# Decode attention with a cached KV: products with v moved from VectorE to TensorE

## The chip, the cores and the metric

The kernel runs on one core of a Trainium2 chip. The metric is device time in microseconds, the median of several executions. Profile figures come from one further execution taken with the hardware profiler.

## The reference

One token passes four layers: attention, MLP, attention, MLP, both attention layers over the same cache and with the same weights. All is float32: D = 640, 32 heads of 128, 8192 cached positions, 1728 hidden units.

```python
def _A_ref(x, k_cache, v_cache, wq, wo):        # k_cache, v_cache: 1 x 32 x 8192 x 128
    q = (x @ wq).reshape(B, Sq, H, Dh).transpose(0, 2, 1, 3)
    scores = jnp.einsum("bhqd,bhkd->bhqk", q, k_cache) * (Dh ** -0.5)
    p = _softmax(scores, axis=-1)
    o = jnp.einsum("bhqk,bhkd->bhqd", p, v_cache)
    return o.transpose(0, 2, 1, 3).reshape(B, Sq, H * Dh) @ wo
def _B_ref(x, w1, w2):
    return jnp.einsum("bsf,fd->bsd", jnp.maximum(jnp.einsum("bsd,df->bsf", x, w1), 0), w2)

x = x + _A_ref(_layernorm(x), k_cache, v_cache, wq, wo)
x = x + _B_ref(_layernorm(x), w1, w2)
x = x + _A_ref(_layernorm(x), k_cache, v_cache, wq, wo)
x = x + _B_ref(_layernorm(x), w1, w2)
```

## The kernel before

The cache, 268 MB, has to be streamed once for each attention layer. Every head's 8192 positions are laid out as four row groups (32 partitions each) by 2048 columns, and a head is cut into units of columns (`PARTS`, mostly two of 1024; 1024 columns are 4 MB of k and v). All units go through one ring of 3712 columns in SBUF. `pump` issues the next unit's DMA on SyncE's queue (SP) as soon as `place` finds a free stretch, and `release` frees a unit when it has been used. Layer 1 goes through the heads backwards and starts with the units that are still in the ring (`KEPT`), which are loaded only once. SP also issues the weights, in its order of the program: the query weights `wq` and the output weights `wo` of each group of four heads (1280 KB each, one buffer each), and in layer 0 `w1` and `w2`.

For a unit, `scores` (L263) multiplies q, repeated over 32 weight columns, with the keys: four matmuls for 512 columns, one for each row group. VectorE takes the rows' minimum of the negated scores (L272), ScalarE takes the exponential in place in PSUM with its running sum (L274). `values` (L289) is then one VectorE pass for each quarter of the head's 128 dimensions: v, stored with dimensions in the rows, times the exponentials, summed along the row; four passes a unit. A program order written by hand interleaves four of these passes with the next unit's scores and with `chores`, generators that are advanced a step at a time: `heads_out` (rescale four heads' partial sums by their maxima, L304 to L351, then `times_rows` with wo, L239), `queries` of the next group (L220 to L234), and near the end of a layer `mixing` and `before_last`.

`mixing` prepares the product of the last head's part of wo (centred) with `w1`, so that the last head's output `c_o` (L581) can go directly into the MLP's hidden row: it turns that part of wo (L366), centres it (L382, L384) and multiplies it with w1 in four quarters (L397, L404). It starts at the third head from the end. `before_last` adds the first 31 heads to x and multiplies with w1 (L410). After the last unit the rest of the layer follows: the last head's weights by its maxima (L523 to L549), c_o, the hidden row, ReLU, w2 (L239), and x2 (L648). Units listed in `early` have their scores issued before the unit ahead of them is finished.

Of the kernel before, what the change touches and what calls it, by code (L numbers as in the profile page):

```python
# [15 lines left out]
P = 128  # L16
D = 640
# [14 lines left out]
UNIT = 1024  # L32
# [5 lines left out]
RING = 3 * UNIT + 640  # L38
KEPT = [(30, 2), (30, 3), (31, 0), (31, 1), (31, 2), (31, 3)]
# [9 lines left out]
def decode_kernel(ctx: ExitStack, tc: tile.TileContext, x, kv, wq, wo, w1, w2, out):  # L49
# [5 lines left out]
    ps_s = ExitStack()  # L55
    ctx.enter_context(ps_s)

    def cut_banks(n):

        ps_s.close()  # L60
        pool = tc.tile_pool(name=f"ps_{n}", bufs=4 // n, space=bass.MemoryType.PSUM)
        banks[:] = [ps_s.enter_context(pool), n * 512]

    def bank_tile():
        return banks[0].tile([P, banks[1]], F32, name="ps")

    banks = []
    cut_banks(2)
    ctx.enter_context(tc.manual_schedule())
# [4 lines left out]
    order = [(h, i) for h in range(H) for i in range(len(PARTS[h]))]  # L74
    assert KEPT == order[len(order) - len(KEPT) :]
    todo = [(0, s) for s in order] + [(1, s) for s in order[::-1][len(KEPT) :]]
    dram_at = {}
    for h, i in order:
        dram_at[h, i] = (h * COLS + sum(PARTS[h][:i])) * 8 * P
    live = {}  # L80

# [9 lines left out]
    def pump():  # L91
        while todo:
            layer, (h, i) = todo[0]
            n = PARTS[h][i]
            at = place(n)
            if at is None:
                return
            todo.pop(0)
            live[layer, (h, i)] = at, n
            o = dram_at[h, i]  # L100
            nc.sync.dma_start(
                ring[:, 8 * at : 8 * (at + n)],
                kv[o : o + 8 * P * n].rearrange("(p m) -> p m", p=P),
            )

    def key(layer, s):
        return (0, s) if s in KEPT else (layer, s)

    def release(layer, s):
        if layer or s not in KEPT:  # L110
            del live[key(layer, s)]
            pump()
# [3 lines left out]
    def load_wq(g):  # L116
        wq_t[g] = wts.tile([P, NB, HG * DH], F32, name="wq_t")
        nc.sync.dma_start(wq_t[g], wq[g])

    def load_wo(g):  # L120
        wo_t[g] = wts.tile([P, HG, D], F32, name="wo_t")
        nc.sync.dma_start(wo_t[g], wo[g])
# [3 lines left out]
    load_wq(0)  # L126
    pump()
    load_wo(0)

    ones = consts.tile([P, P], F32, name="ones")  # L130
# [10 lines left out]
    fold = consts.tile([P, 32], F32, name="fold")  # L141
    nc.vector.tensor_reduce(fold, ident.rearrange("p (g d) -> p d g", g=4), AX.X, ALU.add)
    all_rows = sel[:, 4:5].to_broadcast([P, P])
# [5 lines left out]
    junk = ps_m.tile([P, UNIT], F32, name="junk")  # L149
# [35 lines left out]
    def spread_of_columns(xc):  # L185
# [6 lines left out]
        nc.tensor.matmul(pv, ones, ss, start=True, stop=True)  # L192
# [22 lines left out]
    def queries(g, xc, r):  # L215

        pq = ps_m.tile([P, 512], F32, name="pm")
# [12 lines left out]
        pt = ps_m.tile([P, 512], F32, name="pm")  # L230
# [17 lines left out]
    st = {}  # L248
    probs = {}

    def scores(step, run):

        L, s, n, e = step
        at, _ = live[key(L, s)]
        nm, _ = st[run[0]]
        j = run.index(s[0])
        ps = bank_tile()
        q = qT[s[0] // HG][:, s[0] % HG : s[0] % HG + 1].to_broadcast([P, 32])
        for b in range(0, n, 512):
            d = min(n, b + 512)  # L260
            for g in range(4):
                k = 8 * at + g * n
                nc.tensor.matmul(  # L263
                    ps[32 * g : 32 * g + 32, b:d],
                    q,
                    ring[:, k + b : k + d],
                    start=True,
                    stop=True,
                )
        probs[L, s] = ps[:, :n]  # L270
        yield
        nc.vector.tensor_reduce(nm[:, j, e : e + 1], ps[:, :n], AX.X, ALU.max, negate=True)  # L272
        yield
        nc.scalar.activation(  # L274
            ps[:, :n],
            ps[:, :n],
            AF.Exp,
            bias=nm[:, j, e : e + 1],
            scale=1.0,
            accum_out=st[run[0]][1][:, 0, j, e : e + 1],  # L280
        )

    def values(step, run, hi):

        L, s, n, e = step
        at, _ = live[key(L, s)]
        j = run.index(s[0])
        v = 8 * at + (4 + hi) * n
        nc.vector.scalar_tensor_tensor(  # L289
            junk[:, :n],  # L290
            ring[:, v : v + n],
            1.0,
            probs[L, s],
            op0=ALU.mult,
            op1=ALU.mult,
            accum_out=st[run[0]][1][:, 1 + hi, j, e : e + 1],
        )

    def heads_out(run, acc, first, last):

        nm, lo = st.pop(run[0])
        J, n = nm.shape[1], nm.shape[2]
        low = work.tile([P, J], F32, name="c_low")
        nc.vector.tensor_reduce(low, nm, AX.X, ALU.min)  # L304
        pt = ps_m.tile([P, 512], F32, name="pm")
        for g in range(4):
            nc.tensor.matmul(  # L307
                pt[:, g * J : (g + 1) * J],
                sel[:, g : g + 1].to_broadcast([P, P]),
                low,  # L310
# [4 lines left out]
        all_low = work.tile([P, J], F32, name="c_all")  # L315
        nc.vector.tensor_reduce(
            all_low, pt[:, : 4 * J].rearrange("p (g j) -> p j g", g=4), AX.X, ALU.min
        )
        d = work.tile([P, J, n], F32, name="c_d")
        nc.vector.tensor_tensor(  # L320
            d, nm, all_low[:, :, None].to_broadcast([P, J, n]), op=ALU.subtract
        )
        w = work.tile([P, J * n], F32, name="c_w")
        nc.scalar.activation(w, d.rearrange("p j e -> p (j e)"), AF.Exp, bias=0.0, scale=-1.0)
        yield
        t = work.tile([P, 5, J * n], F32, name="c_t")
        nc.vector.tensor_tensor(
            t,
            lo.rearrange("p i j e -> p i (j e)"),
            w[:, None, :].to_broadcast([P, 5, J * n]),  # L330
            op=ALU.mult,
        )
        sums = work.tile([P, 5, J], F32, name="c_s")
        nc.vector.tensor_reduce(  # L334
            sums, t.rearrange("p i (j e) -> p i j e", j=J), AX.X, ALU.add
        )
        pt = ps_m.tile([P, 512], F32, name="pm")
        nc.tensor.matmul(pt[:, :J], all_rows, sums[:, 0], start=True, stop=True)  # L338
        for hi in range(4):
            nc.tensor.matmul(  # L340
                pt[32 * hi : 32 * hi + 32, J : 2 * J],
                fold,
                sums[:, 1 + hi],
                start=True,
                stop=True,
            )
        yield
        rl = work.tile([P, J], F32, name="c_r")
        nc.vector.reciprocal(rl, pt[:, :J])
# [375 lines left out]
```

## Time and profile before

| | |
|---|---|
| time, median of 3 runs | 1440.14 us (1439.71 to 1440.53) |
| the profiled execution | 1441.47 us, span 1439.7 us |
| busy: TensorE, its weight loads, VectorE, ScalarE | 618.8, 216.4, 849.8, 170.4 us |
| moved by DMA | 570.78 MB, mean 396 GB/s |
| granted TensorE clock, mean | 0.628 of full |

Rows of the windows view give, for a stretch of time, each engine's busy time, the granted clock, the busy share of the 16 DMA engines and what they moved. Rows of groups give line, engine, operation, out<-in, shapes and count, then busy time, the mean of one in ns, and the idle time before it with what ended it. Rows of the timeline start with the start and the length in us; what ended the idle time before them stands in brackets. A float32 matmul leaves two records in each count.

### The profile page before, as it was taken

To read this page: it belongs to the slowest core of one execution; us is meant where nothing else is said; L and a number is where in the kernel's file an instruction comes from. 1 tells how busy PE (TensorE), PEld (TensorE's weight loads), DVE (VectorE), ACT (ScalarE), POOL (GpSimd) and SP (SyncE) were. 2 spreads that over 40 slices of the span, in tenths; PEclk is the share of its full clock that TensorE was granted. 3 is DMA by queue.
4 is the path that set the end of the run, shared out by engine and by line. 5 is a ranking of instruction groups with operands and counts; after the bars stand their busy time and mean duration, and the time that the engine had idled before them with its cause. 6 is when DMAs were issued, how large, how long until landed. Compare 5 with 4: busy or idle time off the path is not lost. (4 is left out here: it accounts for less than half of the span.)

```text
span 1439.7 us, 10806 instructions
## 1 busy us (share of the span) xinstructions
PE 618.8 (43%) x4140; PEld 216.4 (15%) x4140; DVE 849.8 (59%) x1509; ACT 170.4 (12%) x319; POOL 2.9 (0%) x10
## 2 busy tenths in 40 slices
PE   3343443333434343444574343434434343333476
PEld 1111111011110111112241011111101110111233
DVE  4566566465466655664737756556565665656464
ACT  1111111111111111111101111111111111111110
POOL 0000000000000000000000000000000000000000
PEclk9555665555565566567765665655655656565586
DMA  9999999999999999998517899999999999999980
GB/s 397 438 430 432 428 427 436 428 431 430 431 430 432 432 430 427 435 430 362 217 38 319 359 435 431 429 430 433 432 429 430 432 430 429 431 431 432 429 375 1
DMA packets 24396, 570.78 MB, mean 396 GB/s; under 512 B 2709, under 2 KB 2841, under 8 KB 3097
## 3 DMA queue, kind: packets, MB, share of 16 engines
q1 hardware_dynamic: 24344, 570.09, 92.7%
q8 instruction: 33, 0.54, 0.2%
q14 instruction: 19, 0.15, 0.0%
HBM read 570.08 MB, written 0.00 MB: 396 GB/s over the span
## 5 line engine op out<-in xcount | busy, mean ns | idle before, releaser
L289 DVE SCALAR_TENSOR_TENSOR junk<-ring,ps 128x1024 f32<-128x1024 f32 (+3 forms) x568 | 637.4, 1122 | 203.4 <-ACT ps L274 190.5
L263 PE MATMUL ps<-ring,qT 128*32 128x512 f32 (+1 forms) x2112 | 447.3, 990 | 637.7 <-DMA ring<-in_kv 554.3
L272 DVE TENSOR_REDUCE nm<-ps 128x1 f32<-128x1024 f32 (+4 forms) x142 | 158.8, 1119 | 348.6 <-PE ps L263 348.5
L274 ACT ACTIVATE ps<-ps,nm 128x1024 f32<-128x1024 f32 (+4 forms) x142 | 142.6, 1004 | 1157.2 <-DVE nm L272 1157.2
L263 PEld LDWEIGHTS ps<-ring,qT 128*32 128x32 f32 x2112 | 83.9, 154 | 927.4 <-issue 730.8
L289 DVE DVE_READ_ACCUMULATOR junk<-ring,ps 128x1 f32 x568 | 79.7, 140 | 0.0
L338 PE MATMUL pm<-c_s,sel 128*128 128x4 f32 (+1 forms) x32 | 8.9, 350 | 86.3 <-DVE c_s L334 86.3
L397 PE MATMUL pm<-w_t,wct 128*128 128x448 f32 (+1 forms) x80 | 31.1, 536 | 2.9 <-ACT mix L404 2.4
L220 PE MATMUL pm<-wq_t,ln_xc 128*32 128x128 f32 x640 | 30.4, 356 | 1.7 <-DMA wq_t<-in_wq 1.7
L220 PEld LDWEIGHTS pm<-wq_t,ln_xc 128*32 128x32 f32 x640 | 28.1, 151 | 19.1 <-issue 19.1
L307 PEld LDWEIGHTS pm<-c_low,sel 128*128 128x128 f32 x128 | 23.3, 272 | 31.7 <-issue 31.7
L239 PE MATMUL acc<-wo_t,c_o 128*32 128x160 f32 x496 | 26.9, 373 | 2.8 <-DVE c_o L351 2.8
L307 PE MATMUL pm<-c_low,sel 128*128 128x4 f32 (+1 forms) x128 | 24.7, 316 | 6.7 <-DVE c_low L304 6.7
L274 ACT ACTIVATION_READ_ACCUMULATOR ps<-ps,nm 128x1 f32 x142 | 27.4, 193 | 0.0
L239 PEld LDWEIGHTS acc<-wo_t,c_o 128*32 128x32 f32 x496 | 19.9, 147 | 24.5 <-issue 17.6
L231 PE MATMUL pm<-sel,q_row 128*128 128x4 f32 x32 | 7.5, 304 | 34.0 <-DVE q_row L229 34.0
L338 PEld LDWEIGHTS pm<-c_s,sel 128*128 128x128 f32 x32 | 8.0, 310 | 90.5 <-issue 90.5
L397 PEld LDWEIGHTS pm<-w_t,wct 128*128 128x128 f32 x80 | 14.5, 190 | 20.2 <-issue 11.9
L366 PE MATMUL pm<-ident,wo_t 128*128 128x128 f32 x8 | 2.2, 428 | 28.5 <-DMA wo_t<-in_wo 28.5
L410 PE MATMUL acc<-w_t,ln_xc 128*32 128x448 f32 (+1 forms) x80 | 13.1, 786 | 1.2 <-DVE ln_xc L182 1.2
L239 PE MATMUL junk<-w_t,hT 128*32 128x160 f32 (+1 forms) x224 | 13.2, 388 | 0.0
L231 PEld LDWEIGHTS pm<-sel,q_row 128*128 128x128 f32 x32 | 6.1, 237 | 39.5 <-DVE q_row L229 39.5
(100 smaller groups left out, 118.8 us busy)
## 6 DMA issues: line engine op xcount, KB each, us to landing
ring<-in_kv SPq DMA_DIRECT2D x118, 4096.0 KB, 20.7
wq_t<-in_wq SPq DMA_DIRECT2D x15, 1280.0 KB, 20.4
wo_t<-in_wo SPq DMA_DIRECT2D x15, 1280.0 KB, 17.4
ring<-in_kv SPq DMA_DIRECT2D x7, 2048.0 KB, 14.6
ring<-in_kv SPq DMA_DIRECT2D x8, 1024.0 KB, 10.2
w_t<-in_w SPq DMA_DIRECT2D x1, 4480.0 KB, 30.6
w_t<-in_w SPq DMA_DIRECT2D x1, 4320.0 KB
ring<-in_kv SPq DMA_DIRECT2D x1, 2560.0 KB, 12.6
```

The costliest lines, as they stand in the source:

```text
L220: nc.tensor.matmul(pq[32 * j : 32 * j + 32, :DH], xc[:, c : c + 1].to_broadcast([P, 32]), wq_t[g][:, c, j * DH : (j + 1) * DH], start=(c = ...
L231: nc.tensor.matmul(pt[:, :HG], row, sel[:, :HG], start=True, stop=True)
L239: nc.tensor.matmul(acc[32 * g : 32 * g + 32, :DR], col.to_broadcast([col.shape[0], 32]), wt[:, g * DR : (g + 1) * DR], start=first, stop=last,
L263: nc.tensor.matmul(ps[32 * g : 32 * g + 32, b:d], q, ring[:, k + b : k + d], start=True, stop=True,)
L272: nc.vector.tensor_reduce(nm[:, j, e : e + 1], ps[:, :n], AX.X, ALU.max, negate=True)
L274: nc.scalar.activation(ps[:, :n], ps[:, :n], AF.Exp, bias=nm[:, j, e : e + 1], scale=1.0, accum_out=st[run[0]][1][:, 0, j, e : e + 1],)
L289: nc.vector.scalar_tensor_tensor(junk[:, :n], ring[:, v : v + n], 1.0, probs[L, s], op0=ALU.mult, op1=ALU.mult, accum_out=st[run[0]][1][:, ...
L307: nc.tensor.matmul(pt[:, g * J : (g + 1) * J], sel[:, g : g + 1].to_broadcast([P, P]), low, start=True, stop=True,)
L338: nc.tensor.matmul(pt[:, :J], all_rows, sums[:, 0], start=True, stop=True)
L366: nc.tensor.transpose(pt[:, c * P : (c + 1) * P], wt[:, c * DR : c * DR + P], ident)
L397: nc.tensor.matmul(pt[:, :n], wct[:, c], w1_t[:, c, f : f + n], start=(c == 0), stop=(c == NB - 1),)
L410: nc.tensor.matmul(ph[32 * g : 32 * g + 32, :n], col.to_broadcast([P, 32]), wt[:, f : f + n], start=first, stop=last, skip_group_check=True,)
```

## The change

The exponentials go to SBUF, `turn` brings their keys into the rows with four TensorE matmuls for 512 columns (the exponentials as the 128-column weights, four columns of `sel` moving), VectorE copies the small result, and `values` is 16 matmuls for 512 columns into PSUM (v stored with the keys in the rows; 32 equal weight columns; 128 columns moving). Steps are of at most 512 columns, units hold one or two steps, and each step is released by itself. `combined` rescales one head at a time. `wq` and `wo` are issued on ScalarE's DMA queue after their buffers' last use, and so are `w1`, `w2` (at heads 4 and 7 of layer 0) and a copy of the last head's part of wo (at head 8, in both layers). The mixing starts at head 11, its quarters at heads 12, 16, 20 and 24, one matmul for each step of the list `slow`. First and last units are cut smaller; the ring has the same size.

```diff
-PARTS = {h: [UNIT, UNIT] for h in range(H)}
-PARTS[0] = [256, 256, 512, 1024]
-PARTS[29] = [512, 1024, 512]
-PARTS[30] = [128, 256, 1024, 640]
-PARTS[31] = [1024, 512, 256, 256]
-KEPT = [(30, 2), (30, 3), (31, 0), (31, 1), (31, 2), (31, 3)]
+STEP = 512
+UNITS = {h: [[512, 512], [512, 512]] for h in range(H)}
+UNITS[0] = [[128], [128], [256], [512], [512, 512]]
+UNITS[29] = [[512, 512], [512], [512]]
+UNITS[30] = [[256], [128], [256, 512], [512, 384]]
+UNITS[31] = [[512, 512], [512], [256], [128], [128]]
+KEPT = [(30, 2), (30, 3)] + [(31, i) for i in range(5)]
+MIX_AT = [12, 16, 20, 24]
...
+    def exponentials(st):
+        st.p = work.tile([P, STEP], F32, name="p", bufs=2)
+        nc.scalar.activation(st.p[:, : st.m], st.ps[:, : st.m], AF.Exp, ...)
+    def turn(st):
...
+        for b in range(nb):
+            nc.tensor.matmul(pt[:, 4 * b : 4 * b + 4], st.p[:, b * P : (b + 1) * P],
+                sel[:, :4], start=True, stop=True)
+        st.pT = work.tile([P, STEP // 32], F32, name="pT", bufs=2)
+        nc.vector.tensor_copy(st.pT[:, : 4 * nb], pt[:, : 4 * nb])
+    def values(st):
...
+        for b in range(nb):
+            for g in range(4):
+                v = at + (4 * b + g) * DH
+                nc.tensor.matmul(outs[32 * g : 32 * g + 32, st.slot],
+                    st.pT[:, 4 * b + g : 4 * b + g + 1].to_broadcast([P, 32]),
+                    ring[:, v : v + DH], start=(b == 0), stop=(b == nb - 1), ...)
+        release(st.L, st.s)
...
+    def mixing_quarter(g):
+        for c in range(NB):
+            nc.tensor.matmul(pt[:, :n], wct[:, c], w1_t[:, c, f : f + n], ...)
+            yield
+        nc.scalar.copy(mix[:, f : f + n], pt[:, :n])
...
+        def run_out(k):
+            projected(acc, runs[k], o_cols[k], k == 0, False)
+            yield
+            load_wo(groups[k + 1], nc.scalar)
...
+            if where == 8:
+                nc.scalar.dma_start(mix[:, :D], wo[last // HG][:, last % HG])
+            if where == 11:
+                slow.append(mixing())
+            if where in MIX_AT:
+                slow.append(mixing_quarter(MIX_AT.index(where)))
...
+        for i, unit in enumerate(units):
...
+            work_off(chores, slow)
+            both = i + 1 in ahead and len(unit) + len(units[i + 1]) == 2
+            if i + 1 in ahead:
+                begin(i + 1)
+                if both:
+                    go_on(i + 1)
...
+            for st in unit:
+                turn(st)
+            if i + 1 in ahead and not both:
+                go_on(i + 1)
+            work_off(chores)
+            for st in unit:
+                values(st)
...
+            work_off(chores, slow)
+            if i + 1 not in ahead:
+                begin(i + 1)
+                go_on(i + 1)
```

Here `begin` issues a unit's scores and minima and `go_on` its exponentials. `ahead` holds the last units of a layer (all of the last head's but the first) and the kept units at the start of layer 1.

More of the change, by code (lines that the diff above doesn't have):

```diff
@@ L191, in spread_of_columns @@
         pv = bank_tile()[:, :1]
[L192 removed]
+        nc.tensor.matmul(pv, ss.to_broadcast([P, P]), ones, start=True, stop=True)
         return inv_std(pv)
@@ L246, in times_rows @@
             )
[L248 to L305, printed above, removed]
+    class Step:
+        def __init__(self, L, s, m, e):
+            self.L, self.s, self.m, self.e = L, s, m, e
```

542 lines of the change are left out of this document (283 added, 259 removed).

## The prediction

> **What bounds the kernel now.** I read the page's queues and costliest groups first, then busy time by stage, then the timeline around the stages where transfers thin out.
>
> ```profile
> q1 hardware_dynamic: 24344, 570.09, 92.7%
> ring<-in_kv SPq DMA_DIRECT2D x118, 4096.0 KB, 20.7
> L263 PE MATMUL ps<-ring,qT 128*32 128x512 f32 (+1 forms) x2112 | 447.3, 990 | 637.7 <-DMA ring<-in_kv 554.3
> ```
>
> TensorE idles 637.7 us in front of the scores, 554.3 of them for keys and values to land. A whole 4 MB unit lands 20.7 us after its issue. The stages say where the transfers are not full:
>
> ```profile
> core 0: us, PE busy (x) PEld busy (x) DVE busy (x) ACT busy (x) POOL busy (x), PEclk, DMA share, GB/s
> 0.00:4.00 4.00, 0.77 (x11) 0.77 (x11) 1.13 (x13) 1.28 (x1) 0.70 (x6) 1.00 0.49 141
> 100.00:650.00 550.00, 218.30 (x1410) 69.34 (x1410) 323.84 (x516) 61.73 (x107) 0.00 (x0) 0.60 1.00 431
> 660.00:703.00 43.00, 26.90 (x134) 12.36 (x134) 23.05 (x53) 7.72 (x18) 0.00 (x0) 0.82 0.90 364
> 703.00:757.00 54.00, 36.87 (x368) 19.98 (x372) 28.01 (x102) 5.92 (x18) 1.10 (x2) 0.59 0.08 29
> 757.00:850.00 93.00, 39.64 (x272) 12.04 (x276) 65.51 (x134) 12.90 (x27) 0.00 (x0) 0.61 0.88 367
> 1300.00:1403.00 103.00, 56.02 (x281) 21.91 (x282) 63.62 (x101) 14.06 (x26) 0.00 (x0) 0.68 0.97 414
> 1403.00:1439.70 36.70, 23.74 (x270) 12.75 (x270) 17.52 (x69) 3.52 (x12) 0.55 (x1) 0.69 0.01 2
> 680.00:690.00 10.00, 9.40 (x32) 4.32 (x31) 3.87 (x10) 1.72 (x4) 0.00 (x0) 1.00 0.85 338
> 1410.00:1420.00 10.00, 7.02 (x64) 3.90 (x68) 4.67 (x19) 0.56 (x2) 0.00 (x0) 0.50 0.00 0
> ```
>
> In a full stage the queue moves 431 GB/s at a share of 1.00 while VectorE is busy 59% and TensorE 40%: the stream is the bound and no engine is. Against 431, the time lost (length x (1 - rate/431)) is 2.7 us at the start, 6.7 before layer 0's last byte (660 to 703), 50.4 between the layers (703 to 757), 13.8 while the ring refills (757 to 850), 4.1 before the last byte of all (1300 to 1403) and 36.5 behind it: 114 us. The rest, 1325 us, is bytes, and no part of the change takes bytes away. So the change can win in those 114 us, and lose them and more if an engine becomes slower than the stream.
>
> **The two mixing stalls.**
>
> ```profile
> 665.52 1.09 PE L366 MATMUL pm<-ident,wo_t 128*128 128x128 f32 x4 [19.17 <-DMA wo_t<-in_wo]
> 667.13 0.67 ACT L274 ACTIVATE ps<-ps,nm 128x512 f32<-128x512 f32 x1
> 667.95 0.70 DVE L289 SCALAR_TENSOR_TENSOR junk<-ring,ps 128x512 f32<-128x512 f32 x1 [15.18 <-ACT ps L274]
> 677.64 4.03 PE L397 MATMUL pm<-w_t,wct 128*128 128x448 f32 x10 [0.62 <-ACT mix L404]
> ```
>
> At the third head from the end the mixing wants the last group's wo, which stands in SP's queue behind keys. TensorE waits 19.17 us, the exponential stands behind the mixing's copy on ScalarE, VectorE idles 15.18, nothing is released and the ring starves; then four blocks like the 4.03 us one stand ahead of the scores. The change brings the 320 KB it needs at head 8 and spreads the quarters one matmul at a time over heads 12 to 24. I take away both losses: -6.7 - 4.1 = -10.8 us; at worst (the 4.1 has other parts) -6. The copy is read again in each layer: 2 x 0.33 MB at 431 GB/s, +1.5.
>
> **The unit in the stream.** Per 1024 columns (4096 KB, 9.7 us at 431 GB/s; 10.5 us with an eighth of two weight loads of 1280 KB) VectorE's four products go. TensorE gets eight turning matmuls (weights 128 x 128, four moving columns) and 32 products (32 weight columns, 128 moving).
>
> ```profile
> 398.26 3.64 PE L263 MATMUL ps<-ring,qT 128*32 128x512 f32 x16 [5.17 <-DMA ring<-in_kv]
> 1394.59 1.92 PE L263 MATMUL ps<-ring,qT 128*32 128x512 f32 x16 [1.53 <-DMA ring<-in_kv]
> L307 PE MATMUL pm<-c_low,sel 128*128 128x4 f32 x112 | 21.0, 310 | 0.0
> L599 PE MATMUL ps<-sel,wct 128*128 128x4 f32 x12 | 1.9, 273 | 0.8 <-DVE wct L593 0.8
> L220 PE MATMUL pm<-wq_t,ln_xc 128*32 128x128 f32 x640 | 30.4, 356 | 1.7 <-DMA wq_t<-in_wq 1.7
> 749.32 1.68 PE L220 MATMUL pm<-wq_t,ln_xc 128*32 128x128 f32 x40
> L272 DVE TENSOR_REDUCE nm<-ps 128x1 f32<-128x512 f32 x8 | 5.5, 689 | 3.8 <-PE ps L263 3.8
> L274 ACT ACTIVATE ps<-ps,nm 128x512 f32<-128x512 f32 x8 | 5.3, 664 | 17.9 <-DVE nm L272 17.9
> L274 ACT ACTIVATION_READ_ACCUMULATOR ps<-ps,nm 128x1 f32 x142 | 27.4, 193 | 0.0
> L234 DVE COPY qT<-pm 128x4 f32<-128x4 f32 x16 | 2.5, 156 | 1.4 <-PE pm L231 1.4
> ```
>
> A matmul here leaves two records. Turning has its own shape in L307: 21.0/56 = 0.375 us each, 3.0 a unit; the queries' shape is that of the products: 30.4/320 = 0.095, 3.0 a unit. Scores are 447.3/2112 x 16 = 3.4. With about 1.1 a unit of chores (three wide matmuls a head; queries and output rows every fourth head) that is 10.5 us at the clock of now (0.60), against 10.5 of stream: at that clock TensorE would be even with it. At full clock (1.92 for the scores; L599's 1.9/6 = 0.32 for turning; 0.084 or less for products, from 1.68/20) it is 1.9 + 2.5 + 2.7 + 0.9 = 8.0; wholly cold some 11.3 (10.5 x 3.64/3.4). Within a unit TensorE also waits for an exponential, at most 0.69 + 0.66 + 0.19 = 1.5 us, and as the two steps overlap I take half, 0.7.
>
> Which clock? The rows show that it follows density: 1.00 where TensorE was busy 9.40 of 10 us, 0.50 where 7.02; the same scores took 3.64 us after a wait of 5.17 and 1.92 after one of 1.53. A TensorE that falls behind runs products into scores, over 6 us without a gap, and wakes its clock; then it catches up. I therefore cost the middle of the stream at nothing: 8.7 us hidden by 10.5, with 20.7 - 9.7 = 11 us of queued transfer to cover a late release. Without that cover each 0.1 us a unit costs 12.4 us over 124 loaded units. The Trainium skill speaks against it: its page "TensorE: Matmul & The Clock Gate", section "A second HAM failure mode: psum-queue depth-cycling", says that short idles between groups of matmuls that cycle through PSUM banks let the clock swing between half and full rate, at the cost of warming up again and again. By the dense row a unit takes 8.7 us; by that rule, taken as the middle of warm and cold, about 10.4 (estimate), which leaves the sum as it is but without slack. No run so far shows which holds for this mixture.
>
> VectorE falls to two reductions and two copies a unit (1.7 us), ScalarE stays at two exponentials (1.7): neither binds.
>
> **Weights on ScalarE's queue.** With the share at 1.00 a second queue adds no bandwidth: 0. A load there waits for the matmuls that read the old weights, and exponentials stand behind it; between lie at least eight turning matmuls (3.0 us) against 1.3 of output rows, so 0, and up to 3 us each, 30 times, if not; the 11 us of queue cover that too.
>
> **The two ends.**
>
> ```profile
> 734.26 0.16 DVE L581 TENSOR_TENSOR c_o<-pm,c_r 128x1 f32<-128x1 f32 x1 [0.36 <-PE pm L573]
> 747.29 0.08 DVE L648 DVE_READ_ACCUMULATOR xr<-junk,ln_r,xr 128x1 f32 x1
> 756.84 46.58 SPq L101 DMA_DIRECT2D ring<-in_kv  x8
> 1428.23 0.16 DVE L581 TENSOR_TENSOR c_o<-pm,c_r 128x1 f32<-128x1 f32 x1 [0.36 <-PE pm L573]
> 1436.78 0.08 DVE L648 DVE_READ_ACCUMULATOR xr<-junk,ln_r,xr 128x1 f32 x1
> L410 PE MATMUL acc<-w_t,ln_xc 128*32 128x448 f32 (+1 forms) x80 | 13.1, 786 | 1.2 <-DVE ln_xc L182 1.2
> 730.13 2.45 PE L410 MATMUL acc<-w_t,ln_xc 128*32 128x448 f32 x24
> L239 PE MATMUL acc<-wo_t,c_o 128*32 128x160 f32 x496 | 26.9, 373 | 2.8 <-DVE c_o L351 2.8
> 1421.54 0.16 DVE L523 TENSOR_REDUCE c_low<-nm 128x1 f32<-128x4 f32 x1
> 1422.99 0.20 ACT L549 ACTIVATE c_w<-c_d 128x4 f32<-128x4 f32 x1 [0.89 <-DVE c_d L547]
> ```
>
> From the last byte to the last head's output (c_o) it is now 31.4 us in layer 0 (703 to 734.4) and 25.4 in layer 1; VectorE has 2048 columns or more of products left. Afterwards TensorE has them. The scores of the 512 unit, which stand ahead of the turning of the 1024 before it, start when it lands, 4.9 us before the last byte, or about 3.9 with a signal's delay (my estimate). Then, at mean durations: scores of 1024 columns 3.4; sixteen turnings 6.0; products of 2048 columns 6.1; the head before, three wide matmuls, 1.1; its rows 24/496 x 26.9 = 1.3; layer norm some 1.3 (estimate: three wide matmuls and their hand-overs); the hidden rows 13.1/2 = 6.5; eight wide matmuls for the last head 3.0; two chains from minimum to weight, 1.65 each (1421.54 to 1423.19), 3.3: 32.0, so c_o at +28. At full clock: 1.9 + 5.1 + 5.4 + 1.0 + 1.0 + 1.0 + 2.45 x 5/3 = 4.1 + 2.5 + 3.3 = 25.3, less if products go at the scores' 0.06 (1.5): about +20. I take +23.5, as the stretch is dense but starts cold: -7.9 in layer 0 (from -11.4 to -3.4), -1.9 in layer 1 (from -5.4 to +2.6). From c_o to the layer's end nothing changes but the clock (13.0 and 8.5 us now): 0, within 4.5 either way.
>
> Layer 1's first release comes 9.5 us after the layer's result (747.37); a first unit of 128 columns instead of 256 and one product instead of four shorten that by an estimated 1.5 (0 to 3). The refill then waits on releases: now 13.8 us are lost. The new pieces fit the ring worse: walking the placement rule through its releases, head 29's first piece waits for 896 columns of head 30, and head 28's first for a piece of head 29 that layer 1 itself loaded. With 4.1 us per 512 columns on TensorE (the middle of 4.7 at the clock of now and 3.6 at full clock) I get loads of 128, 256, 512, 512 and 1024 columns at 0, 4.7, 10.4, 17.0 and 26.1 us and of 1024 at 43.7 and 56: 33 us of transfer in 56, 23 lost; with 3.0 (all three passes at the full clock of the scores) 9; I take 16, as nothing waits for a landing there and the clock should rise: +2.2, from -5 to +9.
>
> **Sum.** -10.8 + 1.5 - 7.9 - 1.9 - 1.5 + 2.2 = -18.4. The profiled execution took 1441.5 around its span of 1439.7, 1.3 over the median of 1440.1; from 1441.5 it becomes 1423.1, and against the median 1421.7, the forecast.
>
> **Rivals.** (1) Slower: TensorE becomes the stream's bound. For it: 10.5 us a unit at today's clock before any wait, and a turning matmul moves only four columns, which may not count as density. Against: the 9.40-of-10 row at clock 1.00. It decides from a mean clock of about 0.68 downwards in mid-layer, where the work is 9.8 (between 8.0 at 1.00 and 10.5 at 0.60, linear in 1/clock) and the exponential's wait fills the 10.5. At today's clock a unit takes 11.2: 0.7 x 124 = 87 us, less 18.4, 1509; wholly cold (12.0) 1608; 0.15 a unit eats the gain. The Trainium skill's same page, "Part 4: PE-mode transpose", states that transposes in that mode do not count as busy for the clock gate; turning here is an ordinary matmul, so the rule may not reach it, and no run here shows it. (2) The ends swap VectorE for TensorE one for one, and only the mixing pays: 1440.1 - 10.8 + 1.5 = 1431. For it: the +28 above. (3) No change: the refill eats the rest (16 to 30 us lost in it), or starvation at 660 comes back elsewhere: 1438 to 1443. Against it, head 8's load has eight heads of slack.
>
> **How the numbers follow.** Forecast 0.64, rival (1) 0.17, (2) 0.13, (3) 0.06. All good ends together, -10.8 + 1.5 - 11.4 - 5.4 - 3 - 5 - 4.5 = -38.6, give 1402; all poor ones, -6 + 1.5 - 3.4 + 2.6 + 9 + 4.5 = +8.2, give 1448, and I stop at 1446, which takes in (2) and (3); what is left out is most of rival (1). The forecast's own range is 1402 to 1437. Faster by over 0.2% (2.9 us; about what a measurement of this kernel can tell from no change): 0.63 + 0.13 = 0.76; within it 0.07; slower 0.17.
>
> **What would show it.** Right: 431 GB/s from 100 to 1390 but for the layers' change, no dip at 660 or 1300, a granted clock above 0.65 in the stream with TensorE at 65 to 85%, c_o some 20 to 28 us behind each last byte, TensorE in the chain at the end. Wrong: scores that no longer wait for landings in mid-layer, fewer than 425 GB/s there, exponentials that wait behind ScalarE's transfers, or a refill that loses over 25 us.

## The result, and the profile after

The changed kernel took 1560.22 us (median; 1555.95 to 1568.6) against 1440.32 for the kernel before on the same chip: a ratio of 1.084, 95% interval 1.0795 to 1.0886. It is slower by 120 us; the forecast was 1421.7, faster by 18.4. Rival (1), TensorE as the stream's bound, is what happened. Ratios and their intervals, here and below, leave out executions in a slower state of the chip (one of the run with two banks and one of the control further down), while the medians count them, so a ratio can differ a little from that of the medians.

The page of the kernel after: engines, the stream's queue and the weights' queue, the shares of the chain that ended last, then the costliest TensorE groups (busy us in total, mean ns | idle us before them and what ended it) and the whole units' transfers with their us from issue to landing.

```profile
PE 1263.2 (81%) x14484; PEld 880.2 (57%) x14484; DVE 385.0 (25%) x1350; ACT 223.1 (14%) x617; POOL 2.9 (0%) x10
...
q1 hardware_dynamic: 20456, 524.38, 81.0%
q10 hardware_dynamic: 4608, 46.37, 7.2%
...
PE 72%; DVE 12%; DMA 10%; issue 5%; ACT 2%; SPq 0%; ACTq 0%; DVEq 0%
...
L313 PE MATMUL outs<-ring,pT 128*32 128x128 f32 x8192 | 418.9, 385 | 38.3 <-DVE pT L305 37.5
...
L297 PE MATMUL outs<-sel,p 128*128 128x4 f32 x2048 | 325.5, 281 | 74.3 <-DVE pT L305 41.0
...
L263 PE MATMUL ps<-ring,qT 128*32 128x512 f32 (+3 forms) x2144 | 327.7, 735 | 21.7 <-DMA ring<-in_kv 21.2
...
ring<-in_kv SPq DMA_DIRECT2D x117, 4096.0 KB, 16.4
```

The scores waited 554.3 us for landings before; now it is 21.2. TensorE is busy 81% of the span and carries 72% of the chain: the data is there and TensorE is late. A unit lands 16.4 us after its issue instead of 20.7, so the queue behind the stream is shorter. The stages of the kernel after (us, busy time by engine, granted clock, DMA share, GB/s):

```profile
core 0: us, PE busy (x) PEld busy (x) DVE busy (x) ACT busy (x) POOL busy (x), PEclk, DMA share, GB/s
100.00:640.00 540.00, 438.91 (x5054) 307.58 (x5050) 133.35 (x451) 78.72 (x214) 0.00 (x0) 0.74 0.98 408
...
700.00:900.00 200.00, 159.74 (x1676) 107.85 (x1679) 46.30 (x175) 24.49 (x76) 1.10 (x2) 0.65 0.51 206
900.00:1380.00 480.00, 399.48 (x4706) 278.43 (x4702) 123.62 (x420) 73.77 (x200) 0.00 (x0) 0.76 0.98 409
1380.00:1554.10 174.10, 143.31 (x1640) 99.76 (x1632) 43.85 (x163) 22.73 (x65) 0.55 (x1) 0.72 0.69 282
```

The same cuts of the kernel before, the two that are not at full rate:

```profile
700.00:900.00 200.00, 95.08 (x746) 37.24 (x746) 126.72 (x285) 24.84 (x55) 1.10 (x2) 0.60 0.70 292
...
1380.00:1439.70 59.70, 39.58 (x348) 19.58 (x346) 31.49 (x91) 7.75 (x19) 0.55 (x1) 0.77 0.38 161
```

Time lost, length x (1 - rate/431): 28.8 us from 100 to 640 and 24.5 from 900 to 1380 where the kernel before lost 0 and 3.3 (its 428); 104.4 from 700 to 900 against 64.5; 60.2 behind 1380 against 37.4. So of 113 us (the spans differ by 114.4), 50 arose in the steady middle, 40 around the change of layers and 23 at the end.

What TensorE waited for (total us, times, longest):

```profile
PE pm L373 <- DVE c_o L367: 76.2, 62, 2.1
PE pm L330 <- DVE c_low L328: 55.0, 64, 0.9
PE outs L297 <- DVE pT L305: 41.0, 114, 0.5
PE outs L313 <- DVE pT L305: 37.5, 141, 0.3
PE outs L297 <- ACT p L280: 32.5, 41, 1.7
...
DVE c_o L363 <- PE outs L313: 140.2, 59, 3.0
```

These five make 242 us, 1.9 for each of the 128 units' worth (1024 columns) of keys and values. L330 waits for the minimum of a head's maxima. The two rows that wait for the copy of the turned weights (L305) come from their place in the outputs' bank: the next turning (L297) waits until the first result has been copied out of it, and the products (L313), which write to the same bank, wait for the copy of the second. (With a bank of its own for the turned weights, in the runs with wide turning below, this last wait falls from 37.5 to 5.4 us.) The last row is VectorE: before it reads a head's partial outputs it waits for products that run into the same banks, and the head's two summing matmuls (L373) then wait for VectorE at the front of TensorE's queue.

### The profile page after: what moved, and what is told of

Read it like the earlier page. It is cut to its first block, busy times and chain, and to the rows that moved or that the text cites. A ratio compares the mean times of both kernels' runs of the same rounds, so it can differ in the third digit from the quotient of the medians.

```text
span 1554.1 us, 31963 instructions
## 1 busy us (share of the span) xinstructions
PE 1263.2 (81%) x14484; PEld 880.2 (57%) x14484; DVE 385.0 (25%) x1350; ACT 223.1 (14%) x617; POOL 2.9 (0%) x10
## 4 chain that ended last, share of the span: by engine, by line
PE 72%; DVE 12%; DMA 10%; issue 5%; ACT 2%; SPq 0%; ACTq 0%; DVEq 0%
PE outs L313 25%; PE outs L297 18%; PE ps L263 17%; DMA ring<-in_kv 10%; DVE c_o L367 4%; DVE pT L305 3%; PE px L420 3%; DVE nm L273 2%; PE pm L373 2%; ACT p L280 2%; PE pm L330 1%; DVE c_o L363 1%; PE px L221 1%; PE acc L433 1%; PE px L240 1%
## 5 line engine op out<-in xcount | busy, mean ns | idle before, releaser
L313 PE MATMUL outs<-ring,pT 128*32 128x128 f32 x8192 | 418.9, 385 | 38.3 <-DVE pT L305 37.5
L297 PEld LDWEIGHTS outs<-sel,p 128*128 128x128 f32 x2048 | 310.7, 230 | 177.0 <-ACT p L280 110.3
L297 PE MATMUL outs<-sel,p 128*128 128x4 f32 x2048 | 325.5, 281 | 74.3 <-DVE pT L305 41.0
L313 PEld LDWEIGHTS outs<-ring,pT 128*32 128x32 f32 x8192 | 344.3, 156 | 68.2 <-DVE pT L305 49.8
L263 PE MATMUL ps<-ring,qT 128*32 128x512 f32 (+3 forms) x2144 | 327.7, 735 | 21.7 <-DMA ring<-in_kv 21.2
L280 ACT ACTIVATE p<-ps,nm 128x512 f32<-128x512 f32 (+3 forms) x268 | 179.0, 668 | 1105.8 <-DVE nm L273 1004.0
L273 DVE TENSOR_REDUCE nm<-ps 128x1 f32<-128x512 f32 (+3 forms) x268 | 178.9, 668 | 544.5 <-PE ps L263 544.3
L263 PEld LDWEIGHTS ps<-ring,qT 128*32 128x32 f32 x2144 | 76.4, 136 | 146.7 <-issue 120.7
L305 DVE COPY pT<-outs 128x16 f32<-128x16 f32 (+3 forms) x268 | 46.6, 174 | 393.1 <-PE outs L297 392.6
L373 PE MATMUL pm<-sel,c_o 128*128 128x1 f32 x124 | 29.1, 304 | 76.2 <-DVE c_o L367 76.2
L330 PEld LDWEIGHTS pm<-sel,c_low 128*128 128x128 f32 x128 | 19.4, 191 | 112.9 <-DVE c_low L328 111.3
L373 PEld LDWEIGHTS pm<-sel,c_o 128*128 128x128 f32 x124 | 23.8, 240 | 81.5 <-DVE c_o L367 81.5
L367 DVE SCALAR_TENSOR_TENSOR c_o<-outs,c_w,c_o 128x128 f32<-128x128 f32 x194 | 68.1, 351 | 6.9
L330 PE MATMUL pm<-sel,c_low 128*128 128x4 f32 x128 | 24.9, 265 | 55.0 <-DVE c_low L328 55.0
L280 ACT ACTIVATION_READ_ACCUMULATOR p<-ps,nm 128x1 f32 x268 | 51.7, 193 | 0.0
L420 PE MATMUL px<-w_t,wct 128*128 128x448 f32 (+1 forms) x80 | 47.3, 680 | 0.0
## 6 DMA issues: line engine op xcount, KB each, us to landing
ring<-in_kv SPq DMA_DIRECT2D x117, 4096.0 KB, 16.4
```

The source lines that it names most:

```text
L263: nc.tensor.matmul(st.ps[32 * g : 32 * g + 32, :n], q, ring[:, at + g * n : at + (g + 1) * n], start=True, stop=True,)
L273: nc.vector.tensor_reduce(nm[:, st.e : st.e + 1], st.ps[:, : st.m], AX.X, ALU.max, negate=True)
L280: nc.scalar.activation(st.p[:, : st.m], st.ps[:, : st.m], AF.Exp, bias=nm[:, st.e : st.e + 1], scale=1.0, accum_out=l[:, st.e : st.e + 1],)
L297: nc.tensor.matmul(pt[:, 4 * b : 4 * b + 4], st.p[:, b * P : (b + 1) * P], sel[:, :4], start=True, stop=True,)
L305: nc.vector.tensor_copy(st.pT[:, : 4 * nb], pt[:, : 4 * nb])
L313: nc.tensor.matmul(outs[32 * g : 32 * g + 32, st.slot], st.pT[:, 4 * b + g : 4 * b + g + 1].to_broadcast([P, 32]), ring[:, v : v + DH], st ...
```

## The experiments

**The second queue.** All transfers of weights go back to SP's queue.

```
-            load_wo(groups[k + 1], nc.scalar)
+            load_wo(groups[k + 1], nc.sync)     # and every other nc.scalar.dma_start
```

> The changed kernel with wq, wo, w1, w2 and the copy for the mixing issued on SyncE's queue again. Theory T (TensorE is the bound in mid-layer: about 9.5 us of work a unit at a granted clock of 0.74 and some 2 us of hand-over waits make 11.3 us, against 10.5 of stream): no change, 1545 to 1575 us, and 400 to 405 GB/s from 1000 to 1400 as before. Rival D (the 403 GB/s at a DMA share of 0.97 come from two queues that share the engines): 431 GB/s in mid-layer again and about 1490.

1550.73 us, ratio 1.0772 (1.0732 to 1.0812), and from 1000 to 1400 the same rate as the kernel after, 403 GB/s in both. The second queue is not the cause; at most it costs some 10 us of the 120, as the two runs' ranges (1545.69 to 1557.94, and 1555.95 to 1568.6) just touch. The Trainium skill, page "DMA: Bandwidth & Descriptors", section "Issuing engines are not separate DMA queues", says that transfers issued by different engines share the same DMA engines; the equal rates agree.

**Less work, or fewer waits.** First, half of the turning goes.

```
-        nb = st.m // P
+        nb = max(1, st.m // P // 2)      # in turn(); values() reads column 4 * (b % half) + g
```

> The changed kernel with half of the turning left out: each step turns only its first half of 128-column blocks and uses them for the second half too, so part of the products is taken with the wrong weights. Theory T: turning takes 325 us of TensorE in 268 steps; half of it is about 1.25 us a unit, which brings the unit from 11.3 to about 10.1, under the stream's 10.5: mid-layer back to 425 to 431 GB/s, and 1475 to 1490 us. Rival D (queues): 1550 to 1560, still about 403 GB/s. Rival C (turning lowers the clock because it does not count as dense): more than that, the granted clock rises from 0.74 to above 0.85 and products take about 2 us for 64 records in place of 3.3.

Second, the summing matmuls of a head go one step later, behind other TensorE work:

```
         del heads_of[h]
+        yield
         pt = ps_m...
```

> The changed kernel with one more step between VectorE's rescaling of a head's output and the two matmuls that sum it, so that TensorE does not stand waiting for VectorE. Theory T: TensorE waits 76 us for it in 62 heads, 0.6 us a unit; mid-layer gains most of that, 1500 to 1525 us. Rival C (the clock is what matters): the wait is filled but the clock falls as before, gain under 25 us. Rival D: no change.

Third, the turned weights leave the outputs' bank every other time (one bank fewer for scores):

```
-    turned = [outs[:, SLOTS, 16 * i : 16 * i + 16] for i in range(4)]
+    tr = ps_m.tile([P, 512], F32, name="tr")
+    turned = [tr[:, :16], outs[:, SLOTS, :16]]    # ps_s: bufs 3 -> 2
```

> The changed kernel with the results of turning put alternately into a PSUM bank of their own and into the bank of before (the scores get two banks in place of three for it). Theory T: the second turning of a unit no longer waits for the copy of the first (41.0 us in 114 waits of 0.36 us); as TensorE is the bound, the time falls by about as much: 1515 to 1530 us. Rival: such short waits are covered by others (the next exponential), gain under 15 us.

Fourth, the second and third together:

> The changed kernel with both hand-over edits: the later summing matmuls and turning into two PSUM banks. Theory T: in mid-layer the stream is the bound again with some slack, 428 to 431 GB/s, so this adds less than the two gains apart (72 and 63 us): 1460 to 1475 us. What stays over the early mixing alone (1422) is the layers' ends, where TensorE does products and turning one after another.

The windows 1000 to 1400 of half turning, late output, two banks, and the last two together, in this order:

```profile
1000.00:1400.00 400.00, 306.47 (x3905) 192.81 (x3904) 108.62 (x377) 65.58 (x178) 0.00 (x0) 0.80 1.00 425
```
```profile
1000.00:1400.00 400.00, 334.53 (x4072) 236.03 (x4072) 109.00 (x368) 65.16 (x176) 0.00 (x0) 0.80 1.00 425
```
```profile
1000.00:1400.00 400.00, 343.37 (x4062) 235.93 (x4054) 107.36 (x362) 63.86 (x173) 0.00 (x0) 0.76 0.99 420
```
```profile
1000.00:1400.00 400.00, 331.26 (x4110) 231.93 (x4106) 109.45 (x371) 65.17 (x177) 0.00 (x0) 0.79 1.00 425
```

Half turning took 1464.61 us (ratio 1.0182, 1.0159 to 1.0205), the late output 1487.68 (1.0336, 1.0321 to 1.0352), two banks 1497.12 (1.0381, 1.0361 to 1.0402; the row above is from an execution of 1510.7) and the last two together 1476.7 (1.0264, 1.0236 to 1.0292). Each alone brings the middle from 403 to 420 or more: at 403 a unit with its share of weights (4416 KB) takes 11.2 us where the stream needs 10.5, so 0.7 us less is enough. The clock of half turning rose to 0.80 in this window, short of the 0.85 that rival C named. All three gained more than expected: 96 us and not 70 to 85, 73 and not 35 to 60, 63 and not 30 to 45. That is also more than the 50 us lost in the middle, so a part of it comes from the layers' ends. The late output's gain is not the wait's alone, because the clock in its window is 0.80 where the kernel after has 0.76. The two together gained only 11 more than the late output alone, and just missed the expectation: once the stream is the bound again, the rest is not in the middle.

**Issuing the next scores earlier**, in every unit instead of the last ones of a layer, without and with the late output:

```
+        ahead = set(range(1, len(units)))
         chores, slow = [], []
```

> The changed kernel with every unit in the list ahead: a unit's scores stand before the turning of the unit ahead of it, in the whole of both layers. Theory T: TensorE has the next scores to do while the exponentials are made, so the waits on ScalarE (142 us with the weight loads) and on the minima go; mid-layer back to 425 GB/s or more, 1490 to 1510 us in all, the rest of the loss at the layers' ends. Rival: a unit's buffer is now freed only after the next one has landed, about 9.7 us later than now, which leaves no unit queued: transfers thin out and nothing is gained, 1540 or more.

> The two edits together: every unit ahead, and one step more between VectorE's rescaling and its two matmuls. Theory T: mid-layer is the stream's at 428 to 431 GB/s with slack for TensorE; what stays is the ends, 45 to 50 us over the kernel before: 1475 to 1488 us. If the ends were long only because of single units that wait for their own exponentials, heads 29 and 30 now overlap too and it would be 1465 or less.

1642.35 us (ratio 1.1421, 1.1363 to 1.1479) and 1651.43 (1.1457, 1.1419 to 1.1494): the first as its rival said, the second a miss. The scores of the run without the late output:

```profile
L263 PE MATMUL ps<-ring,qT 128*32 128x512 f32 (+3 forms) x2144 | 363.8, 808 | 244.9 <-DMA ring<-in_kv 244.2 <-DVE qT L235 0.5
...
ring<-in_kv SPq DMA_DIRECT2D x117, 4096.0 KB, 14.7
```

Its scores wait 244.2 us for landings, while the turning and the products that would release the ring stand behind them: the ring has less queued (14.7 us from issue to landing), and an order that fills an exponential's wait opens a longer one.

**The clock.** A prelude to the kernel before, on TensorE alone: 120 turning matmuls (four moving columns), 60 groups of four products, 120 turning matmuls.

> The kernel before with a prelude on TensorE that nothing waits for but a copy: 120 turning matmuls (128 x 128 weights, four moving columns), 60 groups of four products (32 weight columns, 128 moving), 120 turning matmuls. Rival C (turning does not count as dense): in the first stretch the granted clock stays at 0.5 and a turning matmul takes about 0.46 us throughout; in the products it rises to 1.0; in the third stretch it falls back to 0.5. Theory T without C: the clock rises to 1.0 within the first stretch and stays there, 0.26 us a turning matmul.

Its timeline (start, length) with one row for each stretch, and windows within the second and third stretch:

```profile
1.58 51.33 PE L148 MATMUL pm<-sel,ident 128*128 128x4 f32 x240 [1.58 <-DVE mhalf L138]
52.85 15.01 PE L151 MATMUL acc<-ident,sel 128*32 128x128 f32 x480
67.79 49.33 PE L153 MATMUL pm<-sel,ident 128*128 128x4 f32 x240
```
```profile
57.00:65.00 8.00, 8.00 (x304) 8.00 (x296) 0.00 (x0) 0.00 (x0) 0.00 (x0) 1.00 0.02 4
...
70.00:105.00 35.00, 35.00 (x166) 35.00 (x166) 0.00 (x0) 0.00 (x0) 0.00 (x0) 0.50 0.00 0
```

The total, 1536.21 us in one run, contains the prelude. The products run at clock 1.00. Turning, with TensorE busy 35.00 of 35 us, runs at 0.50: a full TensorE does not hold its clock on this shape, 49.33/120 = 0.41 us each.

The first stretch is turning as well, and there the clock column shows 1.00 where 0.5 was expected. The column cannot be used there: the trace holds no clock record before 56.4 us, and where it has none the column reads 1.00. The spacing of the matmuls tells the clock instead. From record to record the first stretch takes 213.3 ns, just as the third does after its clock has fallen at 70.0 us; before that fall the third takes 112.7. The first clock record of the trace is a rise to 1.00, 3.5 us into the products, and the products, at 52.0 ns a record before it, take 27.0 after it. So turning was slow from the start and did not wake the clock in 51 us of unbroken work; the products did.

In the kernel after it looks like this (start, length, last wait):

```profile
1002.55 1.95 PE L313 MATMUL outs<-ring,pT 128*32 128x128 f32 x64 [0.27 <-DVE pT L305]
...
1020.01 1.87 PE L297 MATMUL outs<-sel,p 128*128 128x4 f32 x8
1022.24 1.84 PE L297 MATMUL outs<-sel,p 128*128 128x4 f32 x8 [0.36 <-DVE pT L305]
1024.35 3.64 PE L313 MATMUL outs<-ring,pT 128*32 128x128 f32 x64 [0.27 <-DVE pT L305]
```

The same 64 records of products take 1.95 us where the clock is up and 3.64 behind a cold turning. So the turning was made wide: its four columns repeated 32 times as moving columns, into a bank of its own, of which four columns a block are copied.

```
+    tr = ps_m.tile([P, 512], F32, name="tr")      # ps_s: bufs 3 -> 2
+    wide = sel[:, None, :4].to_broadcast([P, 32, 4])
-                pt[:, 4 * b : 4 * b + 4],  ...  sel[:, :4],
+                tr[:, P * b : P * b + P],  ...  wide,
```

> The changed kernel with each turning matmul given 128 moving columns (the same four, 32 times) in place of four, into one bank of its own; only four are copied, the result is the same. It makes turning dense at the price of more columns. Rival C (it is the sparse turning that cools the clock): the granted clock in mid-layer rises from 0.76 to 0.9 or more, products fall from a mean of 51 ns a record to about 32, and though turning is no shorter the time falls to 1480 to 1510 us. Theory T without C (only waits and the amount of work count): the clock stays at 0.72 to 0.78, turning gets longer and the time is 1560 to 1620 us.

The control keeps bank and copy, and moves four columns:

```
-                tr[:, P * b : P * b + P],  ...  wide,
+                tr[:, P * b : P * b + 4],  ...  sel[:, :4],
```

> The wide turning had two edits in it: the bank of its own and the 128 moving columns. Here the bank stays and the moving columns are four again; nothing else differs. If the columns did it through the clock: a mean clock of 0.73 to 0.76, products of 385 us or more instead of 263.8, 410 to 422 GB/s from 1000 to 1400, and 1500 to 1535 us, as the run with two places for the turned weights took 1497.1 and this one has a single place with a wait of about 40 us for its copy. If the bank did it: 1460 to 1470 us with the wide clock.

Wide, then the control:

```profile
L297 PE MATMUL tr<-sel,p 128*128 128x128 f32 x2048 | 325.6, 305 | 76.4 <-DVE pT L305 40.5 <-ACT p L281 35.6
...
L316 PE MATMUL outs<-ring,pT 128*32 128x128 f32 x8192 | 263.8, 281 | 6.3 <-DVE pT L305 5.4 <-DVE wct L577 0.8
...
1000.00:1400.00 400.00, 299.97 (x4136) 197.51 (x4136) 107.98 (x368) 65.39 (x177) 0.00 (x0) 0.92 1.00 426
```
```profile
L296 PE MATMUL tr<-sel,p 128*128 128x4 f32 x2048 | 332.8, 285 | 72.2 <-DVE pT L304 40.7 <-ACT p L280 31.2
...
L315 PE MATMUL outs<-ring,pT 128*32 128x128 f32 x8192 | 405.2, 376 | 6.3 <-DVE pT L304 5.4 <-DVE wct L576 0.8
...
1000.00:1400.00 400.00, 344.70 (x3947) 235.81 (x3946) 103.50 (x350) 61.29 (x166) 0.00 (x0) 0.73 0.97 408
```

Wide: 1460.38 us (ratio 1.0147, 1.0131 to 1.0163), better than expected. Control: 1540.39 (1.0631, 1.0571 to 1.0691), just over its expectation. The rows of waits are alike; the moving columns alone are worth 80 us by the medians and 70 by the ratios. 32 times as many columns cost no more time (325.6 against 332.8), and not only because the clock is higher: at a clock of 1.00 four turning matmuls take 1.05 us wide (the wide run at 1014.71) and 1.03 narrow (the kernel after at 1001.26). The products, which are the same instructions in both runs, fall from 405.2 to 263.8, with the clock at 0.92 in place of 0.73. This pair shows the clock as a cause; the bank of its own, with four columns, is worth only the 20 us (30 by the ratios) between the control and the kernel after.

**What the ends cost.** The wide turning with the late output, and that with the pieces (256 columns at the smallest) of the kernel before:

> Wide turning and the later summing matmuls together. With C: TensorE has slack in mid-layer (431 GB/s), the ends get shorter by the warmer clock: 1445 to 1470 us. Without C: about 1490 to 1540.

```
-UNITS[31] = [[512, 512], [512], [256], [128], [128]]
+UNITS[31] = [[512, 512], [512], [256], [256]]     # heads 0 and 30 likewise; six kept pieces
```

> The wide turning with the late output reader took 1455.5 us, 33 more than the early mixing alone, most of it at the layers' ends. Here it gets the pieces of the first and the last two heads back from the kernel before (256 columns at the smallest instead of 128, six kept pieces instead of seven). If the small pieces cost what they cost in the kernel with the early mixing alone (10 us), 1443 to 1448. If the TensorE tail needs them, each piece of 256 adds a later start of its last products, 1456 to 1465.

1455.47 us (ratio 1.011, 1.0096 to 1.0125) and 1441.76 (1.0006, 0.9994 to 1.0019), first the new pieces, then the old:

```profile
700.00:900.00 200.00, 151.73 (x2130) 103.60 (x2122) 56.62 (x212) 30.60 (x91) 1.10 (x2) 0.87 0.70 288
...
1380.00:1454.00 74.00, 56.12 (x651) 36.99 (x650) 17.72 (x75) 7.91 (x25) 0.55 (x1) 0.76 0.36 153
```
```profile
700.00:900.00 200.00, 151.59 (x2140) 103.61 (x2136) 57.50 (x213) 31.35 (x91) 1.10 (x2) 0.90 0.75 311
...
1380.00:1439.00 59.00, 45.81 (x542) 28.52 (x542) 13.79 (x60) 5.81 (x18) 0.55 (x1) 0.80 0.26 111
```

The losses there go from 66.4 + 47.7 to 55.7 + 43.8: 14.6 us, and the medians differ by 13.7, a little more than the 10 that were expected. The small pieces of the change were a cost of their own, most of it in the refill: from the first release to 900 us 19.8 us are lost with the new pieces and 7.4 with the old (373 GB/s from 753, and 409 from 755). With them undone, the clock held and the reader moved, the changed kernel is level with the kernel before; but it has the early mixing in it, so the products on TensorE still eat all that the mixing brings.

**The mixing alone.** The kernel before with the last group's wo copied at head 8 (on SP's queue) and the mixing at head 11; then with smaller ends (128 columns) in the first and the last head; then in the first head only.

```
-                if where == H - 3:
+                if where == 8:
+                    nc.sync.dma_start(mix[:, :D], wo[last // HG][:, last % HG])
+                if where == 11:
                     chores.append(mixing(last))

-PARTS[0] = [256, 256, 512, 1024]
+PARTS[0] = [128, 128, 256, 512, 1024]     # second and third run
-PARTS[31] = [1024, 512, 256, 256]
+PARTS[31] = [1024, 512, 256, 128, 128]    # second run only, KEPT + (31, 4)
```

> The kernel before with one part of the change alone: the copy of the last head's wo is loaded at head 8 and the mixing is done from head 11 on, w1 and w2 at heads 4 and 7; all on SyncE's queue, products still on VectorE. My prediction's term: 10.8 us lost at 660 to 703 and 1300 to 1403 come back, 1.5 are paid for the copy: about 1431 us, and no dip in transfers before a layer's last byte. Rival: the dips come from the ring's shape at the end of a layer, not from the mixing: 1440 to 1443.

> The kernel before with early mixing (1422 us) and, as in the change, the last 256 columns of head 0 and of head 31 cut into two units of 128. It asks whether the smaller last units are worth something where VectorE does the products. The work that VectorE has left after the last byte is the same, each further unit adds some 1.5 us of fixed costs to it, and the first release of layer 1 comes about 1.5 us earlier: 1420 to 1426 us.

> The early mixing alone, with smaller pieces in the first head only (128, 128, 256, 512, 1024), so that what the last head's pieces and the longer kept list cost stays out. If the refill of the ring was what the smaller ends lost, 1419 to 1424 us; if the short pieces themselves cost (more instructions on VectorE at the end of layer 1), 1427 to 1432.

The mixing alone took 1422.43 us (ratio 0.9876, 0.9862 to 0.9891), about 9 better than the 1431 expected; with smaller ends in both heads 1432.68 (0.9955, 0.9942 to 0.9968; a miss), and in the first head only 1423.98 (0.9885, 0.987 to 0.99). Two windows of the mixing alone, and the last row of its layer 0 output:

```profile
1300.00:1385.00 85.00, 35.12 (x202) 9.53 (x194) 53.16 (x82) 11.05 (x19) 0.00 (x0) 0.60 0.99 426
1385.00:1421.00 36.00, 22.48 (x260) 13.26 (x260) 17.05 (x69) 2.69 (x10) 0.55 (x1) 0.67 0.03 10
```
```profile
721.01 0.16 DVE L583 TENSOR_TENSOR c_o<-pm,c_r 128x1 f32<-128x1 f32 x1 [0.36 <-PE pm L575]
```

The dip at 1300 is gone (426 GB/s where 414 were), and since VectorE is no longer behind when the last byte lands, c_o follows it by 23.7 us in layer 0 (697.5 to 721.2) instead of 31.4. (The stream does not end sharply: the last packets of its queue end at 701.9 here and at 704.8 in the kernel before, and from those c_o follows by 19.2 us instead of 29.6.) This is the fastest version, faster than both kernels. The smaller last head and its longer kept list cost most of the 10 us: with the first head's pieces alone, 1.5 remain, which is hardly more than the runs scatter.

## Why the prediction was wrong

**The step that failed** is "I therefore cost the middle of the stream at nothing: 8.7 us hidden by 10.5". It cost 50 us there. The work term was right: 9.3 us of TensorE a unit (333.47 busy of 400 us from 1000 to 1400, x 11.2), where I had 9.2 at that window's clock of 0.76 by my own line. In part that is luck, because the line's end for the full clock was too slow: its row at 749.32 ran at a clock of 0.73, and at 1.00 the products of a unit take 1.95 us (the row at 1002.55) where I had 2.7. Two things beside the work term were wrong.

First, the waits. I counted the exponential alone and took 0.7 us a unit. It measured 0.25 (32.5/128). Four hand-overs with VectorE that I did not count measured 1.6: two for the place of the turned weights in the outputs' bank, one for the combining of a head's outputs, and one for the minimum of its maxima. Taking away the largest (late output) returns the stream to 425 GB/s.

Second, the clock. I argued that "a TensorE that falls behind runs products into scores ... and wakes its clock; then it catches up". TensorE did fall behind, and the clock stayed at 0.74 to 0.76: the turning between them lets it fall however dense it is (probe), so falling behind had no end. Rival (1) named the reason, "which may not count as density", and I gave it 0.17; but its threshold of 0.68 was too low, because its wait was. With 1.9 us of waits 8.6 are left of 10.5, which by my line between 8.0 at 1.00 and 10.5 at 0.60 asks for a clock of about 0.86; wide turning has 0.92 and streams at 426. Either remedy alone brings the stream back (425 GB/s with the late output, 426 with wide turning), so the runs do not divide the 50 us between waits and clock. The rival's price, 1509 at the old clock, put 87 us on the middle, where 50 were measured, and nothing on the layers' change and the end, where 63 were.

The Trainium skill, page "TensorE: Matmul & The Clock Gate", section "A second HAM failure mode: psum-queue depth-cycling", has the clock swing between half and full rate, and the trace agrees (1.00 from 1002.5 to 1004.5 us, 0.50 from 1020 to 1028); the 10.4 (estimate) that I drew from it is to be set against 9.3 of work and 1.9 of waits. The short idles that it gives as the reason are not what holds the clock down here: wide turning and its control have nearly the same waits (76.4 and 72.2 us before turning, 6.3 before the products in both) and clocks of 0.92 and 0.73, and the probe cools without a gap. Its "Part 4: PE-mode transpose" speaks of transpose mode; the probe shows the same for an ordinary matmul with four moving columns, at 0.50.

**The ends.** I forecast c_o 23.5 us behind each last byte; it is 45.5 in layer 0 (737.6 to 783.1) and 33.9 in layer 1 (1504.1 to 1538.0):

```profile
746.83 1.06 PE L263 MATMUL ps<-ring,qT 128*32 128x512 f32 x8
...
782.92 0.16 DVE L616 TENSOR_TENSOR c_ol<-pm,c_r 128x1 f32<-128x1 f32 x1 [0.68 <-PE pm L612]
...
1505.48 1.06 PE L263 MATMUL ps<-ring,qT 128*32 128x512 f32 x8
...
1537.80 0.16 DVE L616 TENSOR_TENSOR c_ol<-pm,c_r 128x1 f32<-128x1 f32 x1 [0.68 <-PE pm L612]
```

From those scores to c_o are 36.2 and 32.5 us, against 32.0 in my sum at mean durations: that sum was near, and my step down toward the full clock was not, as the clock there is 0.71 and 0.72. The stretch also starts 9.2 and 1.4 us after the last byte and not 3.9 before it, since TensorE comes in with a backlog. In layer 0 that goes with the clock: counted from the last packet, the same scores start 7.6 us after it in the kernel after (746.8 against 739.2), 8.4 after it in the control (741.5 against 733.1), but 1.9 before it with wide turning (705.8 against 707.7). With the late output alone it is still 6.6 after. From that packet to c_o the control takes 44.0 us and wide turning 29.4.

**The refill** was sized at 16 us lost, bounds 9 to 23. The first 97 us of it:

```profile
803.00:900.00 97.00, 79.86 (x830) 54.56 (x825) 22.72 (x76) 13.55 (x39) 0.00 (x0) 0.62 0.67 269
```

That is 36.5 us lost. The clock is a part of it, since the same pieces lose 22.7 us with wide turning (330 GB/s from 759 to 856, clock 0.89) and 35.6 in its control (273 from 799 to 896, clock 0.61). The pieces are another part: the old ones take 12.4 us off the refill of the wide turning with the late output.

**Right:** the second queue at nothing (same rate without it); the first release, 7.6 us after the layer's result (795.3 to 802.89) and 9.5 before, -1.9 where I had -1.5; the direction of the mixing, though -9.3 with the copy's bytes was undersized: -17.2 (1439.6 to 1422.4). The sum had only the two dips; c_o also comes 7.7 us sooner behind the last byte in layer 0, as VectorE's backlog goes with the dip.

**Open:** what stays between the best of the products on TensorE (1441.76) and the mixing alone (1422.43). The rates put about 11 us of the 19 into the change of layers and the end (55.7 + 43.8 against 52.4 + 36.3), and some 5 into the middle, where the best of the products has 428 and 429 GB/s (100 to 640, 900 to 1380) and the mixing alone 431 and 430; why the middle is that little slower is not traced. Nor was it tried whether the single row of waits L330 can be taken out.

## What to carry to other kernels

Before work moves to an engine that is busy 40%, count every hand-over that the new instructions add, not only the producer that they wait for: a bank that a reader on one engine shares with a writer on another becomes a wait per unit, and five waits under 0.7 us each can take the whole margin. Do not count on an overloaded TensorE to raise its own clock (here it stayed at 0.74 to 0.76); ask what share of its time goes to matmuls with few moving columns, and widen them if their time does not grow. When a change bundles several edits, cost and run the one with no new bound by itself: here it was the whole gain.

## What was not expected of the hardware

Back-to-back matmuls with 128 x 128 float32 weights and four moving columns let the granted clock fall to 0.50 at 70.0 us, 2.2 after the stretch began, and keep it there with TensorE busy without a gap. In the stretch at the probe's start they did not raise it in 51 us either. With 128 moving columns the same number of records took the same time (325.6 us against 332.8) and the mean clock of the run rose from 0.713 to 0.895.

A reading of 1.00 in the clock column says nothing before the trace's first clock record, which stands at 56.4 us in the probe and at 34.8 in the kernel after. Check the duration of a known matmul there.
